# Heads 0 to 3 leave attention undivided, and GpSimd scales them in the gathered rows of the expert layer

## The chip, the cores and the metric

One core of a Trainium2 chip. The metric is the device time of one execution in microseconds (us). TensorE (PE; its weight loads PEld), VectorE (DVE), ScalarE (ACT), GpSimd (POOL) and SyncE (SP) each run their own instructions in order and wait for one another by semaphores; DMA queues move data between DRAM and the core's SBUF.

## The reference

Attention over keys and values that are averaged in groups of 8, then a mixture of 8 experts in which each token takes the one with the largest logit:

```python
k_p = k.reshape(B, H, Sp, pool, D).mean(axis=3)          # B=8, H=8, S=576, D=64, pool=8, Sp=72
v_p = v.reshape(B, H, Sp, pool, D).mean(axis=3)
scores = scale * np.matmul(q, k_p.transpose(0, 1, 3, 2))
scores = scores - np.max(scores, axis=-1, keepdims=True)
attn = np.exp(scores)
attn = attn / (np.sum(attn, axis=-1, keepdims=True) + 1e-09)
x = np.matmul(attn, v_p)                                  # then (4608 tokens) x (512 = 8 heads x 64)
...
logits = x @ w_gate + modality_bias[modality_id]
e_idx = np.argmax(logits, axis=1)                         # softmax of the logits gives gate_w
for e in range(E):                                        # E=8, w1 512x1024, w2 1024x512
    mask = e_idx == e
    h = np.maximum(x[mask] @ w1[e], 0.0)
    out[mask] = gate_w[mask, None] * (h @ w2[e])
```

## The kernel before

**Attention** (about the first 190 us) works on tiles of 128 tokens, 36 in all, in 20 steps: sixteen steps of two tiles, and four "mixed" steps of one tile that holds the last 64 tokens of two batches. For a tile PE computes the scores of all heads (L520, L526, tile sc), DVE takes the maximum and subtracts it (L533, L536, tile sb), ACT exponentiates (L548, L549, tile pe), PE transposes the result in four pieces (L555, tile pp) and a fifth (L567, 16 columns of each pair of heads), ACT copies these to SBUF (L560 pt, L574 pt4), and PE multiplies with the averaged values (a_pe, L590 and L594) into av: for each head 64 columns of the unnormalized output, 8 columns of the unnormalized routing logits (the values' operand holds v times w_gate besides v) and one column with the sum of the exponentials. av is two PSUM banks, heads 0 to 3 and 4 to 7, as two tiles. GpSimd averages k and v beforehand (L296 to L298: three folds, "kp", "vp").

x_dve then divides, in two halves: per half of four heads a tensor_scalar that takes the sum (L610, r), a reciprocal (L612), a product for the 64 columns of each head into the row tile (L614, xb) and one for the logits (L616, lg). Rows go to a DRAM tensor xs, 528 columns a token: 512 of x, then 16 spare ones of which the routing later writes some (the gate's weight).

v_gate (L382 to L387) builds the operand's part with w_gate for a batch: PE into sc, ACT masks two parts (L385, L386), and DVE a third (L387, tile vw4x), which the next mixed step's attention needs. v_operand (L359 to L361) does it for the values; L361 is on GpSimd from the second batch on.

**The order of the work** is written by hand in a loop over the steps n: transposes and exponentials of the step before's first tile (t_pe, t_act), s_act(n, 0), s_pe(n, 1), the fifth transposes with their copies (t4), a_pe of the first old tile, s_dve(n, 1), t_pe of the second old tile, q_pe(n+1, 1), x_dve of the first old tile, s_act(n, 1), s_pe(n+1, 0), s_dve(n+1, 0), a_pe and x_dve of the second old tile, and hooks between them where k, v, v_gate and the first weight splits stand. gap() releases a few small routing operations on DVE ("drip": the logits' maximum and sum, ranks in L717 and so on) between two such operations. So a tile's x_dve at the end of a step is followed on ACT, in program order, by t_act of the next step.

**The expert layer** works on slots of 256 tokens of one expert, about 23 us each, from about 190 us on: gather (L142, GpSimd's DMA queue) takes the slot's rows from xs by index, two tiles of 128 rows, four buffers xg; x_transposes (L153) turns them, ACT and DVE split them in a high and a low part (L155, L156); for each of 8 chunks f of the hidden dimension PE forms hp (L162) and the output (L1143) while DVE and ACT split the weights (L135, L138) that have been loaded. The rows of slot s+1 are gathered at f = 0 of slot s and transposed at f = 5 (slot 1 into 2: gathered at f = 3, transposed at f = 6). The first two slots are gathered inside attention, from a table for its early tokens, and the weights of the first slot are split there.

Of the kernel before, what the change touches and what calls it, by code (L numbers as in the profile page):

```python
# [22 lines left out]
P = 128  # L23
# [7 lines left out]
def kernel(  # L31
# [25 lines left out]
    XW = D + 16  # L57
    NSTAT = NTOK // SLOT
# [87 lines left out]

    def x_transposes(s, xgs, tts=(0, 1)):
        a, b = xh[s % len(xh)], xl[s % len(xl)]
        for tt in tts:
            x = xgs[(2 * s + tt) % len(xgs)]  # L150
            pt = ps_tr.tile([P, ND, P], F32, tag="tr", name=f"xt_{s}_{tt}")
            for d in range(ND):
                nc.tensor.transpose(pt[:, d, :], x[:, d * P:(d + 1) * P], ident)  # L153
# [29 lines left out]
    with ExitStack() as actx:  # L183
# [82 lines left out]
        nc.gpsimd.iota(m_i, pattern=[[-1, NPAIR]], base=P, channel_multiplier=1)  # L266
        nc.vector.tensor_single_scalar(m_i, m_i, NPAIR - 1, op=ALU.bitwise_and)
# [106 lines left out]
        def v_gate(b):  # L374
# [6 lines left out]
            for u in range(2):  # L381
# [5 lines left out]
            nc.vector.tensor_tensor(d4[:, :, HD:HD + E], pg[:, 2, :].rearrange("p (j e) -> p j e", j=NPAIR),  # L387
                                    m4b.to_broadcast([P, NPAIR, E]), op=ALU.mult)
# [151 lines left out]
        def s_act(n, w):  # L540
# [6 lines left out]
            tail = pe[:, 2 * NPAIR * P:].rearrange("p (t s c) -> p t c s", t=2, c=NPAIR)[:, 0:nt, 2 * w:2 * w + 2, :]  # L547
# [28 lines left out]
        def a_pe(t):  # L576
# [3 lines left out]
            av = [ps_av.tile([P, 512], F32, tag=f"av{u}", name=f"av_{t}_{u}") for u in range(2)]  # L580
# [5 lines left out]
            for u in range(2):  # L586
                for gg in range(2):
                    c = 2 * u + gg
                    for hs, y in halves:
                        nc.tensor.matmul(av[u][hs, 2 * VC * gg:2 * VC * (gg + 1)], pt[:, c, hs],  # L590
                                         vw[y][:, c].rearrange("p a x -> p (a x)"), start=(gg == 0), stop=False)
                dst4 = av[u][:, 0:4 * VC].rearrange("p (g x) -> p g x", g=2)[:, :, VC:2 * VC]
# [3 lines left out]
        def x_dve(t):  # L596
# [9 lines left out]
            for u in range(2):  # L606
                avv = av[u][:, 0:4 * VC].rearrange("p (h x) -> p h x", h=4)
                r = ap.tile([P, 4], F32, tag="r", bufs=4, name=f"r_{t}_{u}")
                rb = r.rearrange("p (h o) -> p h o", o=1)
                nc.vector.tensor_scalar(r, avv[:, :, VC - 1], float(POOL), 1e-9 * POOL, op0=ALU.mult, op1=ALU.add)  # L610
                gap(1)
                nc.vector.reciprocal(r, r)  # L612
                gap(1)
                nc.vector.tensor_tensor(xo[:, u * D // 2:(u + 1) * D // 2].rearrange("p (h d) -> p h d", h=4), avv[:, :, 0:HD],  # L614
                                        rb.to_broadcast([P, 4, HD]), op=ALU.mult)
                nc.vector.tensor_tensor(lgs[g][:, gi, 4 * u:4 * u + 4, :], avv[:, :, HD:HD + E],  # L616
                                        rb.to_broadcast([P, 4, E]), op=ALU.mult)
# [139 lines left out]
        def early_table():  # L757
# [31 lines left out]
            ops += [lambda: [gather(s, gidx0, 2 * s, xg, T_EARLY * P) for s in range(EARLY_SLOTS)]]  # L789
# [323 lines left out]
    def part(s):  # L1113
# [62 lines left out]
        def run(fs, tail):  # L1176
            for f in fs:
# [113 lines left out]
```

## Time and profile before

| | us |
|---|---|
| runs shown: median | 640.91 |
| runs shown: all | 640.91, 641.08, 639.33 |
| the profiled execution's own time | 639.47 |
| its span | 637.8 |
| time around the span | 1.67 |

| engine | busy us | share of the span |
|---|---|---|
| PE | 601.1 | 94% |
| DVE | 433.8 | 68% |
| ACT | 343.8 | 54% |
| POOL | 198.9 | 31% |

The busy shares are averages over two stages: attention, in which DVE is close to full for long stretches, and the expert layer, in which PE is. A time line row has the start, the duration, the engine, the line, the operation with its tiles out<-in, and in brackets the idle time ahead of it with what ended it. A row of the groups has the count, the busy time, the mean in ns, and the engine's idle time just ahead with its releasers.

### The profile page before, as it was taken

The numbers are of one execution on the slowest core, as the hardware profiler recorded it, in microseconds if no ns is written. First come the engines' busy times: TensorE is split into PE (matmuls) and PEld (weight loads), VectorE is DVE, ScalarE is ACT, GpSimd is POOL, SyncE is SP. The second block draws the span as 40 slices with busy tenths as digits, with TensorE's granted clock in tenths as the row PEclk, the third lists the DMA queues.
The fourth block names the chain that finished last, engine by engine and source line by source line (L and its number), as shares of the span: only waits on it lengthen the run. The fifth ranks groups of instructions, "written<-read, shape, count | busy, mean of one in ns | idle before, by whom it ended". The sixth has DMA issues, their size and how long they took to land.

```text
span 637.8 us, 12547 instructions
## 1 busy us (share of the span) xinstructions
PE 601.1 (94%) x4223; PEld 544.8 (85%) x4223; DVE 433.8 (68%) x940; ACT 343.8 (54%) x640; POOL 198.9 (31%) x277
## 2 busy tenths in 40 slices
PE   4799898989899999999999999999999999999992
PEld 3699797888798999999999999999999999999881
DVE  4778989999977578666566566656656566656541
ACT  2667566677441455555555555555556555555530
POOL 6689967563000221320320221231131231131230
PEclk9899999999999999999999999999999999999997
DMA  9999979764201901201210461220225410120120
GB/s 255 290 300 337 350 208 362 223 202 143 67 35 51 315 33 36 68 34 35 68 41 28 148 201 51 67 65 8 63 75 180 145 55 17 52 68 18 51 75 17
DMA packets 63406, 77.18 MB, mean 121 GB/s; under 512 B 15455, under 2 KB 42079, under 8 KB 63328
## 3 DMA queue, kind: packets, MB, share of 16 engines
q1 hardware_dynamic: 57168, 55.98, 28.4%
q0 software_dynamic: 6160, 20.26, 9.7%
q8 instruction: 38, 0.62, 0.4%
q14 instruction: 40, 0.33, 0.2%
HBM read 119.94 MB, written 19.45 MB: 219 GB/s over the span
## 4 chain that ended last, share of the span: by engine, by line
PE 76%; DVE 13%; DMA 7%; issue 1%; ACT 1%; SPq 0%; DVEq 0%; ACTq 0%
PE op L1143 30%; PE hp L162 30%; DMA out_dram<-ob,sidx 6%; PE av L590 3%; PE sc L526 3%; PE xt L153 2%; DVE mx L533 2%; DVE sb L536 2%; PE av L594 2%; DVE xb L614 2%; PE pq L501 1%; PE ph L162 1%; PE pp L555 1%; DVE arow L717 1%; DMA k<-in_k_dram 1%
## 5 line engine op out<-in xcount | busy, mean ns | idle before, releaser
L135 ACT CAST hl<-raw 128x1024 fp32r<-128x1024 f32 x138 | 144.8, 1049 | 138.6 <-PE op L1143 136.6
L162 PE MATMUL hp<-xh,hl 128*128 128x256 f32 x1152 | 186.2, 284 | 0.6 <-issue 0.6
L162 PEld LDWEIGHTS hp<-xh,hl 128*128 128x128 f32 x1152 | 166.0, 189 | 11.5 <-issue 1.0
L138 DVE TENSOR_TENSOR hl<-raw,hl 128x1024 fp32r<-128x1024 f32 x144 | 174.8, 1215 | 0.0
L1143 PE MATMUL op<-hl,hh 128*128 128x512 f32 x554 | 173.5, 394 | 0.0
L1129 POOL DMA_INDIRECT out_dram<-ob,sidx x37 | 51.0, 1379 | 369.3 <-DVE ob L1125 260.2
L166 DVE SCALAR_TENSOR_TENSOR hlo<-hp,hh 128x256 fp32r<-128x256 f32 x139 | 58.8, 423 | 136.6 <-ACT hh L164 136.6
L1143 PE MATMUL op<-hl,hlo 128*128 128x512 f32 x277 | 108.4, 391 | 0.0
L1143 PEld LDWEIGHTS op<-hl,hh 128*128 128x128 f32 x554 | 94.8, 189 | 12.1
L162 PE MATMUL hp<-xl,hl 128*128 128x256 f32 x576 | 92.0, 282 | 0.0
L164 ACT ACTIVATE hh<-hp 128x256 fp32r<-128x256 f32 x139 | 53.4, 384 | 49.6 <-PE hp L162 49.6
L162 PEld LDWEIGHTS hp<-xl,hl 128*128 128x128 f32 x576 | 79.0, 190 | 0.0
L1143 PEld LDWEIGHTS op<-hl,hlo 128*128 128x128 f32 x277 | 52.0, 188 | 11.8
L590 PE MATMUL av<-vw,pt 128*128 128x146 f32 (+1 forms) x320 | 50.9, 299 | 4.9 <-DVE lg L616 3.7
L142 POOL DMA_INDIRECT xg<-xs,gidx x40 | 44.2, 1105 | 17.1 <-issue 8.9
L590 PEld LDWEIGHTS av<-vw,pt 128*128 128x128 f32 (+1 forms) x320 | 40.3, 183 | 7.9 <-DVE lg L616 4.9
L526 PE MATMUL sc<-kt,qt 128*128 128x144 f32 x256 | 38.3, 294 | 1.5 <-DVE rs L706 1.1
L526 PEld LDWEIGHTS sc<-kt,qt 128*128 128x128 f32 x256 | 34.1, 195 | 2.4 <-DVE rs L706 1.3
L156 DVE TENSOR_TENSOR xl<-xt,xh 128x512 fp32r<-128x512 f32 x38 | 24.5, 684 | 15.5 <-ACT xh L155 15.5
L560 ACT COPY pt<-pp 128x512 f32<-128x512 f32 x36 | 21.1, 586 | 25.4 <-PE pp L555 25.0
L533 DVE TENSOR_REDUCE mx<-sc 128x8 f32<-128x576 f32 (+1 forms) x40 | 27.7, 692 | 10.0 <-PE sc L526 7.6
L614 DVE TENSOR_TENSOR xb<-av,r 128x256 f32<-128x256 f32 x72 | 30.4, 422 | 1.6
(226 smaller groups left out, 710.5 us busy)
## 6 DMA issues: line engine op xcount, KB each, us to landing
raw<-in_moe_w_dram SPq DMA_DIRECT2D x304, 256.0 KB
xs<-xb SPq DMA_DIRECT2D x16, 528.0 KB
k<-in_k_dram SPq DMA_DIRECT2D x7, 1024.0 KB
v<-in_v_dram SPq DMA_DIRECT2D x7, 1024.0 KB
q<-in_q_dram SPq DMA_DIRECT2D x6, 1024.0 KB
q<-in_q_dram SPq DMA_DIRECT2D x4, 512.0 KB
v<-in_v_dram SPq DMA_DIRECT2D x16, 128.0 KB
xs<-xb SPq DMA_DIRECT2D x8, 132.0 KB
```

Source lines behind the costliest of these rows:

```text
L135: nc.scalar.copy(hl[f][:, 0, :], raw[f])
L138: eng.tensor_sub(hl[f][:, 1, :], raw[f], hl[f][:, 0, :].bitcast(F32))
L142: nc.gpsimd.indirect_dma_start(out=xgs[(2 * s + tt) % len(xgs)], out_offset=None, in_=xs[0:rows, :], in_offset=IndirectOffsetOnAxis(idx[:, ...
L162: nc.tensor.matmul(ph, hl[f][:, w, d * P:(d + 1) * P], x[:, d, :], start=(n == 0 and d == 0), stop=(n == 2 and d == ND - 1))
L164: nc.scalar.activation(hh, ph, AF.Relu)
L166: nc.vector.scalar_tensor_tensor(hlo, ph, 0.0, hh.bitcast(F32), op0=ALU.max, op1=ALU.subtract)
L526: nc.tensor.matmul(dst, qt[:, i, :], kt[b % NB][:, :, h * SPL:(h + 1) * SPL], start=True, stop=True)
L533: nc.vector.reduce_max(mx, scv, axis=AX.X)
L590: nc.tensor.matmul(av[u][hs, 2 * VC * gg:2 * VC * (gg + 1)], pt[:, c, hs], vw[y][:, c].rearrange("p a x -> p (a x)"), start=(gg == 0), sto ...
L614: nc.vector.tensor_tensor(xo[:, u * D // 2:(u + 1) * D // 2].rearrange("p (h d) -> p h d", h=4), avv[:, :, 0:HD], rb.to_broadcast([P, 4, H ...
L1129: nc.gpsimd.indirect_dma_start(out=out[:, :], out_offset=IndirectOffsetOnAxis(idx.bitcast(U32), 0), in_=ob, in_offset=None, bounds_check=N ...
L1143: nc.tensor.matmul(o[tt], l[:, ts_], hl[f][:, w, D:2 * D], start=(f == 0 and n == 0), stop=(f == NF - 1 and n == 2))
```

## The change

1. **x_dve** takes both halves at once: one tensor_scalar for eight sums, one reciprocal, whose result is written into the row itself (columns RX = 520 to 527), one product for all eight heads' logits. The columns of heads 0 to 3 are copied by ACT without division; DVE divides heads 4 to 7 alone. A gap(2) follows.
2. av is one tile over two banks.
3. **scale_half** multiplies, on GpSimd and in place, the first 256 columns of a gathered row tile by the four reciprocals that came with the row: two operations a slot, at f = 3 of the slot before (f = 5 in slot 1), and for slots 0 and 1 right behind their gathers.
4. **v_gate**: the third part is copied out of PSUM by ACT (vg4) and multiplied on GpSimd.
5. The load of v4 lists its rows in another order with the mask to match, and the exponentials of the fifth part are written in the order (t c s) instead of (t s c).

```diff
+    RX = D + 8
...
+    def scale_half(s, xgs):
+        for tt in range(2):
+            x = xgs[(2 * s + tt) % len(xgs)]
+            xv = x[:, 0:D // 2].rearrange("p (h d) -> p h d", h=H // 2)
+            nc.gpsimd.tensor_tensor(xv, xv, x[:, RX:RX + H // 2].rearrange("p (h o) -> p h o", o=1).to_broadcast([P, H // 2, HD]),
+                                    op=ALU.mult)
...
-            src = rows_of(v, b).rearrange("(c r) x -> r c x", r=2 * SPL)[P:]
+            src = rows_of(v, b).rearrange("(c r) x -> c r x", r=2 * SPL)[:, P:, :]
...
-        nc.gpsimd.iota(m_i, pattern=[[-1, NPAIR]], base=P, channel_multiplier=1)
-        nc.vector.tensor_single_scalar(m_i, m_i, NPAIR - 1, op=ALU.bitwise_and)
+        nc.gpsimd.iota(m_i, pattern=[[-16, NPAIR]], base=P, channel_multiplier=1)
+        nc.vector.tensor_single_scalar(m_i, m_i, 16 * (NPAIR - 1), op=ALU.bitwise_and)
...
-            nc.vector.tensor_tensor(d4[:, :, HD:HD + E], pg[:, 2, :].rearrange("p (j e) -> p j e", j=NPAIR),
-                                    m4b.to_broadcast([P, NPAIR, E]), op=ALU.mult)
+            vg4 = ap.tile([P, NPAIR, E], F32, tag="vg4", bufs=1, name=f"vg4_{b}")
+            nc.scalar.copy(vg4, pg[:, 2, :].rearrange("p (j e) -> p j e", j=NPAIR))
+            nc.gpsimd.tensor_tensor(d4[:, :, HD:HD + E], vg4, m4b.to_broadcast([P, NPAIR, E]), op=ALU.mult)
...
-            tail = pe[:, 2 * NPAIR * P:].rearrange("p (t s c) -> p t c s", t=2, c=NPAIR)[:, 0:nt, 2 * w:2 * w + 2, :]
+            tail = pe[:, 2 * NPAIR * P:].rearrange("p (t c s) -> p t c s", t=2, c=NPAIR)[:, 0:nt, 2 * w:2 * w + 2, :]
...
-            av = [ps_av.tile([P, 512], F32, tag=f"av{u}", name=f"av_{t}_{u}") for u in range(2)]
+            av = ps_av.tile([P, 2, 512], F32, tag="av", name=f"av_{t}")
...
-            for u in range(2):
-                avv = av[u][:, 0:4 * VC].rearrange("p (h x) -> p h x", h=4)
-                r = ap.tile([P, 4], F32, tag="r", bufs=4, name=f"r_{t}_{u}")
-                rb = r.rearrange("p (h o) -> p h o", o=1)
-                nc.vector.tensor_scalar(r, avv[:, :, VC - 1], float(POOL), 1e-9 * POOL, op0=ALU.mult, op1=ALU.add)
-                gap(1)
-                nc.vector.reciprocal(r, r)
-                gap(1)
-                nc.vector.tensor_tensor(xo[:, u * D // 2:(u + 1) * D // 2].rearrange("p (h d) -> p h d", h=4), avv[:, :, 0:HD],
-                                        rb.to_broadcast([P, 4, HD]), op=ALU.mult)
-                nc.vector.tensor_tensor(lgs[g][:, gi, 4 * u:4 * u + 4, :], avv[:, :, HD:HD + E],
-                                        rb.to_broadcast([P, 4, E]), op=ALU.mult)
+            avv = av[:, :, 0:4 * VC].rearrange("p u (h x) -> p u h x", h=4)
+            s8 = ap.tile([P, 2, 4], F32, tag="r", bufs=4, name=f"r_{t}")
+            r = xw[:, z, RX:RX + H].rearrange("p (u h) -> p u h", u=2)
+            rb = r.rearrange("p u (h o) -> p u h o", o=1)
+            nc.vector.tensor_scalar(s8, avv[:, :, :, VC - 1], float(POOL), 1e-9 * POOL, op0=ALU.mult, op1=ALU.add)
+            gap(1)
+            nc.vector.reciprocal(r, s8)
+            gap(1)
+            nc.vector.tensor_tensor(lgs[g][:, gi].rearrange("p (u h) e -> p u h e", u=2), avv[:, :, :, HD:HD + E],
+                                    rb.to_broadcast([P, 2, 4, E]), op=ALU.mult)
+            nc.scalar.copy(xo[:, 0:D // 2].rearrange("p (h d) -> p h d", h=4), avv[:, 0, :, 0:HD])
+            nc.vector.tensor_tensor(xo[:, D // 2:D].rearrange("p (h d) -> p h d", h=4),
+                                    avv[:, 1, :, 0:HD], rb[:, 1].to_broadcast([P, 4, HD]), op=ALU.mult)
+            gap(2)
...
+            ops += [lambda: [gather(s, gidx0, 2 * s, xg, T_EARLY * P) for s in range(EARLY_SLOTS)],
+                    lambda: [scale_half(s, xg) for s in range(EARLY_SLOTS)]]
...
+                if f == (5 if s == 1 else 3) and nxt:
+                    scale_half(s + 1, xg)
                 if f == (6 if s == 1 else 5) and nxt:
                     x_transposes(s + 1, xg)
```

What stands on VectorE for the first old tile of step 7 (tile 9; xb5 is its row tile, r_9 its sums, lg_1 its group's logits; lgr, m1, m2 and oh are dripped routing operations), before:

```order
L610 TENSOR_SCALAR r_9_0_1056<-av_9_0_1030 128x4 [waits PE_49]
L666 TENSOR_REDUCE m1_0_989<-lgr_0_987 128x9 [waits DVE_49]
L612 RECIPROCAL r_9_0_1056<-r_9_0_1056 128x4 [waits DVE_49]
L669 TENSOR_TENSOR lgr_0_987<-lgr_0_987,m1_0_989 128x72 [waits DVE_49]
L614 TENSOR_TENSOR xb5_172<-av_9_0_1030,r_9_0_1056 128x256 [waits DVE_49]
L616 TENSOR_TENSOR lg_1_1055<-av_9_0_1030,r_9_0_1056 128x32
L610 TENSOR_SCALAR r_9_1_1064<-av_9_1_1031 128x4 [waits PE_49]
L673 SCALAR_TENSOR_TENSOR lgr_0_987<-lgr_0_987,w8_166 128x72 [waits Activation_49]
L612 RECIPROCAL r_9_1_1064<-r_9_1_1064 128x4 [waits DVE_49]
L674 TENSOR_REDUCE m2_0_990<-lgr_0_987 128x9 [waits DVE_49]
L614 TENSOR_TENSOR xb5_172<-av_9_1_1031,r_9_1_1064 128x256 [waits DVE_49]
L616 TENSOR_TENSOR lg_1_1055<-av_9_1_1031,r_9_1_1064 128x32
```

And in the change, the same tile on the same engine:

```order
L620 TENSOR_SCALAR r_9_1016<-av_9_991 128x8 [waits PE_49]
L678 TENSOR_REDUCE m1_0_950<-lgr_0_948 128x9 [waits DVE_49]
L622 RECIPROCAL xb5_172<-r_9_1016 128x8 [waits DVE_49]
L681 TENSOR_TENSOR lgr_0_948<-lgr_0_948,m1_0_950 128x72 [waits DVE_49]
L624 TENSOR_TENSOR lg_1_1015<-av_9_991,xb5_172 128x64 [waits DVE_49]
L627 TENSOR_TENSOR xb5_172<-av_9_991,xb5_172 128x256 [waits Activation_49]
```

Eight operations have become four, two routing operations that stood inside the tile stand behind it, and the product of heads 4 to 7 (L627) waits for ACT.

On ACT at the end of step 6 and the start of step 7, before (v_gate's two masks, then step 7's pt copy, exponentials and pt4 copies):

```order
L385 ACTIVATE vw1_138<-sc_6_1_1011,m_a_141 128x4x8 [waits PE_49]
L386 ACTIVATE vw1_138<-sc_6_1_1011,m_b_142 128x4x8
L560 COPY pt_11_1137<-pp_11_1132 128x512 [waits PE_49,Activation_49]
L548 ACTIVATE pe_7_1139<-sb_7_0_1092 128x256 [waits DVE_49]
L549 ACTIVATE pe_7_1139<-sb_7_0_1092 128x2x16
L574 COPY pt4_0_135<-sc_7_0_1076 64x128 [waits PE_49,Activation_49]
```

And in the change:

```order
L393 ACTIVATE vw1_138<-sc_6_1_972,m_a_141 128x4x8 [waits PE_49]
L394 ACTIVATE vw1_138<-sc_6_1_972,m_b_142 128x4x8
L396 COPY vg4_3_1055<-sc_6_1_972 128x32
L626 COPY xb5_172<-av_10_1058 128x256 [waits DVE_49,PE_49]
L569 COPY pt_11_1090<-pp_11_1085 128x512 [waits PE_49,Activation_49]
L557 ACTIVATE pe_7_1092<-sb_7_0_1048 128x256
L558 ACTIVATE pe_7_1092<-sb_7_0_1048 128x32
L583 COPY pt4_0_135<-sc_7_0_1032 64x128 [waits PE_49,Activation_49]
```

Two copies have come in ahead of step 7's pt copy; that of the row tile (L626) waits for VectorE's logits product of the same tile (L624).

On GpSimd in the change, at the same v_gate:

```order
L306 TENSOR_TENSOR kp4_4_935<-k4_4_594 64x64 [waits PE_49,Pool_49]
L369 TENSOR_TENSOR vw41_140<-vp4_3_814,m_4_143 128x4x64
L397 TENSOR_TENSOR vw41_140<-vg4_3_1055,m_4_143 128x4x8 [waits Activation_49]
L304 TENSOR_TENSOR v_4_478<-v_4_478 128x2x256 [waits DMAHW1_49]
L305 TENSOR_TENSOR v_4_478<-v_4_478 128x2x128 [waits Pool_49]
```

The second of the two products (L397) is new and waits for ACT's copy vg4; before, the folds of v stood directly behind the first (L361 there).

More of the change, by code (lines that the diff above doesn't have):

```diff
@@ L788, in early_table @@
             ops += finish_table(lambda: psm["t"], C, gidx0, sidx0, "t0")
-            ops += [lambda: [gather(s, gidx0, 2 * s, xg, T_EARLY * P) for s in range(EARLY_SLOTS)]]
+            ops += [lambda: [gather(s, gidx0, 2 * s, xg, T_EARLY * P) for s in range(EARLY_SLOTS)],
+                    lambda: [scale_half(s, xg) for s in range(EARLY_SLOTS)]]
             return ops
```

4 lines of the change are left out of this document (2 added, 2 removed).

## The prediction

> **What bounds the kernel now.** The windows view comes first: for each stretch the span's microseconds, then the busy time of PE, PEld, DVE, ACT and POOL, then clock and DMA.
>
> ```profile
> 56.00:75.00 19.00, 16.23 (x130) 14.20 (x128) 18.63 (x59) 11.60 (x34) 17.67 (x27) 1.00 1.05 365
> 75.00:86.00 11.00, 10.77 (x105) 9.83 (x104) 10.16 (x43) 5.82 (x15) 5.28 (x9) 1.00 0.75 234
> 86.00:116.00 30.00, 27.19 (x214) 24.23 (x213) 28.36 (x89) 20.10 (x55) 24.22 (x40) 1.00 0.96 309
> ...
> 127.00:139.00 12.00, 10.28 (x78) 9.19 (x78) 11.71 (x27) 9.16 (x24) 10.71 (x19) 1.00 0.68 219
> ...
> 147.00:175.00 28.00, 23.65 (x222) 21.26 (x222) 27.13 (x93) 15.74 (x42) 4.24 (x4) 1.00 0.35 108
> ...
> 203.00:592.00 389.00, 389.00 (x2578) 353.96 (x2577) 244.47 (x359) 211.24 (x311) 82.28 (x66) 1.00 0.24 78
> ```
>
> From 203 to 592 TensorE is busy in all of 389.00 us: nothing that VectorE gives up there is worth anything. Four stretches of attention are different: PE is short of full by 2.77, 2.81, 1.72 and 4.35 us, together 11.65, while VectorE is busy in 95 to 98% of them. So **at most 11.65 us** can be won from a lighter VectorE, in 89 us of the span. Between those stretches (75 to 86) PE leads, and there a late ScalarE costs. The groups of instructions (busy us, mean ns, then the engine's idle time ahead) and the waits (total, times, longest) say who holds PE:
>
> ```profile
> L590 PE MATMUL av<-vw,pt 128*128 128x146 f32 (+1 forms) x320 | 50.9, 299 | 4.9 <-DVE lg L616 3.7 <-DVE r L610 0.8 <-ACT pt L574 0.2
> L614 DVE TENSOR_TENSOR xb<-av,r 128x256 f32<-128x256 f32 x72 | 30.4, 422 | 1.6
> L616 DVE TENSOR_TENSOR lg<-av,r 128x32 f32<-128x32 f32 x72 | 12.9, 179 | 0.0
> L612 DVE RECIPROCAL r<-r 128x4 f32<-128x4 f32 x72 | 12.6, 175 | 1.5
> L610 DVE TENSOR_SCALAR r<-av 128x4 f32<-128x4 f32 x72 | 10.8, 151 | 2.9 <-PE av L594 2.9
> L387 DVE TENSOR_TENSOR vw<-sc,m 128x32 f32<-128x32 f32 x7 | 1.3, 182 | 0.4 <-ACT vw L386 0.3
> L361 POOL TENSOR_TENSOR vw<-vp,m 128x256 f32<-128x256 f32 x7 | 4.2, 607 | 7.0 <-PE pk L332 7.0
> L370 ACT COPY vt<-pv 128x256 f32<-128x256 f32 x8 | 2.9, 368 | 0.1
> ```
>
> ```profile
> PE sc L520 <- DVE vw L387: 3.5, 3, 1.3
> ```
>
> x_dve (L610 to L616) holds PE's next attention product for 3.7 us, the gate product in v_gate (L387) its mixed scores for 3.5. Both are edited.
>
> **The change, part by part.** *x_dve.* Its busy time was 2 x (151 + 175 + 422 + 179) = 1.85 us a tile. Now there is one r of 151, one reciprocal of 175, one logits product of 64 columns instead of 32 (not in the trace; between 179 and 422 by the rows, taken as 0.21, nearest the 32-column row) and one product of 422: 0.96. VectorE is rid of **0.89 us a tile**; ScalarE gets a 128x256 copy out of PSUM (368, by L370). But busy time isn't what PE waits for. One tile in which no other operation stood between the steps:
>
> ```profile
> 145.43 0.15 DVE L610 TENSOR_SCALAR r<-av 128x4 f32<-128x4 f32 x1
> ...
> 145.61 0.18 DVE L612 RECIPROCAL r<-r 128x4 f32<-128x4 f32 x1
> ...
> 145.82 0.42 DVE L614 TENSOR_TENSOR xb<-av,r 128x256 f32<-128x256 f32 x1
> ...
> 146.16 0.18 DVE L616 TENSOR_TENSOR lg<-av,r 128x32 f32<-128x32 f32 x1
> ...
> 147.10 1.22 DVE L138 TENSOR_TENSOR hl<-raw,hl 128x1024 fp32r<-128x1024 f32 x1
> ```
>
> Starts follow each other by 0.18 to 0.34, and the tile takes 1.67 from its first start to that of the next thing. After, by the order, the logits product is followed by ScalarE's copy, and VectorE's product of heads 4 to 7 waits for that copy, since all three touch one row tile: 0.18 + 0.21 + 0.21 + the copy 0.37 with some 0.03 on each side + 0.34 = 1.37. The lock step leaves **0.30 of the 0.89**, and with routing operations dripped into the gaps, which fill them before as after, some 0.1. How many tiles lie in the four stretches, the reciprocal of L612 tells, two to a tile (windows of that line alone):
>
> ```profile
> 56.00:75.00 19.00, 1.18 (x7) 1.00 1.05 365
> 86.00:116.00 30.00, 1.87 (x11) 1.00 0.96 309
> 127.00:139.00 12.00, 0.52 (x3) 1.00 0.68 219
> 147.00:175.00 28.00, 1.75 (x10) 1.00 0.35 108
> ```
>
> 31 are 15.5 tiles. I let a dozen count, since elsewhere a max, a table or a PE chain ends last: 12 x 0.1, **-1.2 us**.
>
> *The copy's place on ScalarE.* A step boundary that PE sets:
>
> ```profile
> 54.55 0.60 PE L555 MATMUL pp<-ident,pe 128*128 128x128 f32 x4
> ...
> 55.24 0.59 ACT L560 COPY pt<-pp 128x512 f32<-128x512 f32 x1 [1.71 <-PE pp L555]
> ...
> 56.40 0.55 ACT L574 COPY pt<-sc 64x128 f32<-64x128 f32 x2
> ...
> 57.90 0.27 PE L555 MATMUL pp<-ident,pe 128*128 128x128 f32 x1
> ```
>
> ScalarE sat idle for 1.71 and began the pt copy 0.69 after the attention product before it had ended; two exponentials and the pt4 copies (L574) come behind, on which the next attention product's last part waits, and the boundary lasts 3.35. Now the xb copy stands ahead of that pt copy: it can begin at 0.18 + 0.21 + 0.21 and a hop, some 0.65 after the same point, and ends at 1.02, so all that follows is 0.33 later. With a dripped routing operation ahead of it, more. The pt copies and exponentials leave PE as much to do as it needs at about six of the sixteen boundaries (the kernel has sixteen steps of two tiles), those of the windows between the four stretches: 6 x 0.3 = **+1.8**. At the others VectorE is later than that anyway.
>
> *v_gate.* L387 leaves VectorE (182 ns, x7), ScalarE copies 128x32, and GpSimd multiplies right behind L361. PE waited for L387 because it stood behind other VectorE work; now it waits for a ScalarE copy (under 0.37, by L370) and a GpSimd product (under 0.61, by L361). That is between -3.5 and, if GpSimd is in a 1.27 us fold, +2; GpSimd gets nothing new ahead of it, for it now stands waiting. This waiting has a second result. VectorE's operations on SBUF were long where GpSimd worked beside them:
>
> ```profile
> 109.22 0.60 POOL L361 TENSOR_TENSOR vw<-vp,m 128x256 f32<-128x256 f32 x1
> ...
> 109.33 1.80 DVE L669 TENSOR_TENSOR lgr<-lgr,m 128x72 f32<-128x72 f32 x1
> ...
> 111.62 0.77 PE L590 MATMUL av<-vw,pt 128*128 128x146 f32 x4 [1.31 <-DVE lg L616]
> ```
>
> ```profile
> 154.63 0.23 DVE L669 TENSOR_TENSOR lgr<-lgr,m 128x72 f32<-128x72 f32 x1
> ```
>
> ```profile
> 131.05 2.29 DVE L717 TENSOR_SCALAR arow<-iota_b,rkf 128x128 bf16<-128x128 bf16 x2
> 131.29 0.60 POOL L361 TENSOR_TENSOR vw<-vp,m 128x256 f32<-128x256 f32 x1
> ...
> 131.86 1.26 POOL L296 TENSOR_TENSOR v<-v 128x512 f32<-128x512 f32 x1
> ...
> 136.22 0.77 PE L590 MATMUL av<-vw,pt 128*128 128x146 f32 x4 [1.13 <-DVE lg L616]
> ```
>
> The same L669 took 1.80 beside GpSimd's work and 0.23 without; the two PE waits that follow are 1.31 and 1.13. In the order of the change GpSimd stands still at its gate product from L361 until ScalarE's copy, a few microseconds later, so these operations lose most of their neighbours, and GpSimd makes the folds up later, where it had 7.0 us of waiting. I take **-2.3**, bounds -4 and 0. The Trainium skill, "SBUF — State Buffer", section "Who interferes with whom", has a VectorE instruction with two SBUF inputs and a GpSimd instruction that reads SBUF exclude each other, the second to issue standing still until the first ends; the 1.80 against 0.23 agrees. By that rule each of the four early scales, below, could hold back a weight split for its whole 0.61: an estimate of 2.4 instead of the 0.65 that the sum takes, which would then be +1.5.
>
> *scale_half.* Two GpSimd products of 128x256 a slot, 0.61 each by L361 (bounds 0.61 and 1.27).
>
> ```profile
> L138 DVE TENSOR_TENSOR hl<-raw,hl 128x1024 fp32r<-128x1024 f32 x144 | 174.8, 1215 | 0.0
> ```
>
> ```profile
> 594.40 1.01 POOL L142 DMA_INDIRECT xg<-xs,gidx  x1 [0.31 <-DMA out_dram<-ob,sidx]
> ```
>
> ```profile
> 598.80 0.63 PE L153 MATMUL xt<-ident,xg 128*128 128x128 f32 x4 [0.21 <-DMA xg<-xs,gidx]
> ```
>
> In the last slot the transposes already wait 0.21 for their gather, so one scale shows there: +0.65. Most other slots have six chunks between gather and transposes, and nothing shows. In all of them a scale may meet L138, but PE leads and VectorE idles in 37% of that stretch: 0. Slot 2, gathered late, gets +0.1. Slots 0 and 1 are scaled at about 157 to 160, in a stretch that VectorE bounds and in which L138 runs: half of one L138, **+0.65** (0 to +2.6, the four scales laid against it). Together **+1.4**.
>
> The two-bank av tile makes PE wait once for the whole tile instead of half by half; the next product is half a step away, except where PE waits already, and this is within the 1.37 above. The load order of v4, the mask and the order of the exponential's tail change no count of instructions: 0, since the loads land steps ahead of their folds and the exponentials keep their size; were the tail's write to take longer or shorter by a few ns, it would be lost in ScalarE's idle time.
>
> Sum: -1.2 + 1.8 - 2.3 + 1.4 = **-0.3 us** on a profiled run of 639.47 (span 637.8). That gives 639.2 in the profile's terms and 640.6 from the median of the runs shown (640.91), which lies 1.4 higher; between the two I say **640.0**, and 637 to 643 for this case alone.
>
> **The rivals.** *Faster, 631.* VectorE's load counts and not its chain: 15.5 tiles less 0.89 each is 13.8 us, more than PE's 11.65 us of idling. If three quarters of that idle time go, -8.7, with the terms of ScalarE and the slots a little smaller than mine, it is about 631. For it: VectorE is busy in 95% and more there, so whatever it sheds lets the next max begin sooner, and its new wait for ScalarE lasts about 0.4 us of each tile's 0.89. Against it: the 4.35 us of the last stretch have tables and weight splits that stay. *Slower, 647.* The lock step is paid at all sixteen boundaries: 16 x (0.33 + a dripped operation of some 0.2) = 8.5, less the 2.3; about 640.9 + 6. It decides where VectorE reaches the logits product later than PE has pp ready (0.69 in the quoted boundary): every microsecond of VectorE's lateness then holds ScalarE's queue as well, which before it did not. For it: ScalarE's pt copy, both exponentials and the pt4 copies all stand behind the copy. Against it: ScalarE is busy in 56 to 76% of the stretches only. *No relief, 642.* The change does not do what it says: VectorE waits for each copy as long as it had worked, the stretches keep their idle time, and +1.8 + 1.4 - 1.2 of the rest stay. *Late slots, 645.* The four early scales and slot 2's come last for their transposes: up to 2.6 + 1.2 + 0.65. The Trainium skill, "GPSIMD Engine Reference", puts GpSimd at about half VectorE's speed for products of two inputs and says to use VectorE; L361's 607 against 422 in L614 is milder than that, and the sum uses 607.
>
> **How the numbers follow.** Forecast 0.43 (of it 0.13 faster by over 0.3%, 0.21 within, 0.09 slower; 0.3% is about what a measurement of this kernel can tell from no change), faster rival 0.27, slower 0.17, no relief 0.08 (within 0.05, slower 0.03), late slots 0.05 (slower). Faster 0.13 + 0.26 = 0.39, with 0.01 of that rival inside 0.3%; within 0.21 + 0.01 + 0.05 = 0.27; slower 0.09 + 0.17 + 0.03 + 0.05 = 0.34. The range 632 to 647 leaves out the far half of the two outer rivals.
>
> **What would show it.** Right: PE's idle time in the four stretches falls by 2 to 4 us, the longest waits for x_dve near 111 and 136 shrink below 0.5; VectorE shows a wait for ScalarE of some 0.4 in most tiles; boundaries such as 54.55 to 57.90 last 3.6 to 3.7; the last slot's transposes wait some 0.8 for GpSimd. The faster rival shows as idle time in the stretches under 4 us and short boundaries; the slower one as PE waits for pt copies or pt4 copies at most boundaries. I am wrong if the copy starts much later than 0.65 after the product, or if routing operations do not shorten when GpSimd stands.

## The result and the profile after

The changed kernel takes **651.14 us** (median of 650.81, 650.9, 651.38, 654.34) against 641.0 for the kernel before (639.33 to 641.48, four runs): a ratio of 1.0168, 95% interval 1.0144 to 1.0191, so 10 to 11 us slower. The prediction said 640.0 with 632 to 647. The profiled execution took 650.9 with a span of 649.2.

The windows of the prediction, from the trace of the change (span's us; busy PE, PEld, DVE, ACT, POOL; clock, DMA):

```profile
56.00:75.00 19.00, 16.39 (x123) 14.53 (x122) 14.07 (x36) 11.57 (x34) 17.59 (x31) 1.00 1.06 322
...
86.00:116.00 30.00, 28.45 (x238) 25.60 (x237) 22.38 (x66) 20.14 (x56) 20.03 (x35) 1.00 0.72 223
127.00:139.00 12.00, 10.79 (x100) 9.14 (x98) 8.43 (x25) 8.75 (x23) 7.74 (x14) 1.00 0.68 181
147.00:175.00 28.00, 24.01 (x205) 21.40 (x203) 23.32 (x68) 20.81 (x57) 12.87 (x19) 1.00 0.52 171
203.00:592.00 389.00, 389.00 (x2571) 352.98 (x2571) 247.05 (x382) 206.94 (x307) 107.21 (x96) 1.00 0.24 78
```

The work in a window is no longer the same, since everything sits some 8 us later, but the shares can be read: VectorE is busy in 74, 75, 70 and 83% of stretches in which it was busy in 98, 95, 98 and 97%. It is unloaded, as the change meant. PE is short of full there by 2.61, 1.55, 1.21 and 3.99 us, 9.36 together where it was 11.65: a relief of 2.29, which is what the prediction named as its sign of being right. The time is worse all the same, since the loss lies outside these windows: from 40 to 56 us PE is busy in 14.32 us where it was in 15.97, and from 175 to 195 in 18.52 where it was in 20.00. The groups of x_dve and of the scales, then the waits (total, times, longest):

```profile
L627 DVE TENSOR_TENSOR xb<-av,xb 128x256 f32<-128x256 f32 x36 | 15.3, 425 | 23.4 <-ACT xb L626 22.9 <-issue 0.5
L626 ACT COPY xb<-av 128x256 f32<-128x256 f32 x36 | 13.4, 373 | 41.2 <-DVE lg L624 29.0 <-issue 4.5 <-PE sc L535 3.9
L624 DVE TENSOR_TENSOR lg<-av,xb 128x64 f32<-128x64 f32 x36 | 8.0, 223 | 0.8
L622 DVE RECIPROCAL xb<-r 128x8 f32<-128x8 f32 x36 | 7.2, 200 | 0.8 <-DMA xs<-xb 0.2
L620 DVE TENSOR_SCALAR r<-av 128x8 f32<-128x8 f32 x36 | 5.9, 163 | 21.9 <-PE av L603 21.9
L152 POOL TENSOR_TENSOR xg<-xg 128x256 f32<-128x256 f32 x38 | 31.7, 837 | 38.6 <-DMA xg<-xs,gidx 38.4
```

```profile
POOL v L304 <- DMA v<-in_v_dram: 8.9, 3, 5.2
...
POOL k L304 <- DMA k<-in_k_dram: 6.2, 2, 4.0
...
PE pq L510 <- DMA q<-in_q_dram: 4.4, 3, 1.9
...
PE av L599 <- DVE xb L627: 1.6, 2, 1.3
```

The same waits for loads before:

```profile
POOL v L296 <- DMA v<-in_v_dram: 7.0, 3, 4.2
...
POOL k L296 <- DMA k<-in_k_dram: 2.9, 2, 1.6
...
PE pq L501 <- DMA q<-in_q_dram: 1.1, 1, 1.1
```

Two things stand out. VectorE's product waits for ScalarE's copy 22.9 us in 35 tiles, 0.65 each. And the loads of the first 60 us are late: the waits for loads listed here are 8.5 us longer together (the engines wait side by side, so this is not time lost). Where the time went is seen from when VectorE begins x_dve of a tile (starts of its first operation, us, with the difference from before; tiles are counted from 0 in order of time; the first 30 us vary by 1 to 2 us between kernels that are alike there):

| tile | before | change | load back | load alone | rows apart | rows together | merged |
|---|---|---|---|---|---|---|---|
| 1 | 31.67 | 37.12 (+5.45) | 30.29 (-1.38) | 35.13 (+3.46) | 34.83 (+3.16) | 29.88 (-1.79) | 32.88 (+1.21) |
| 7 | 57.99 | 65.34 (+7.35) | 57.13 (-0.86) | 66.08 (+8.09) | 68.29 (+10.30) | 59.67 (+1.68) | 59.22 (+1.23) |
| 28 | 155.66 | 163.64 (+7.98) | 155.02 (-0.64) | 163.86 (+8.20) | 165.23 (+9.57) | 157.32 (+1.66) | 150.72 (-4.94) |
| 35 | 190.47 | 202.20 (+11.73) | 194.45 (+3.98) | 198.69 (+8.22) | 200.04 (+9.57) | 192.14 (+1.67) | 185.54 (-4.93) |

In the change 7.35 of the 11.73 us are lost by tile 7, in the first 65 us, before attention has come to the stretches that VectorE bounded. From tile 7 to 28 it moves only 0.63, and then 3.75 more. By 155 us, when 18.2 of VectorE's 22.9 us of waiting for the copy are over, this waiting has shown little in the starts.

The granted clock differs in the early part too. From 20 to 30 us before, then from 20 to 30 and 30 to 40 us in the change (the clock is the third figure from the end):

```profile
20.00:30.00 10.00, 8.03 (x47) 6.66 (x48) 7.19 (x16) 5.16 (x15) 7.23 (x12) 0.83 1.10 306
```

```profile
20.00:30.00 10.00, 10.00 (x55) 9.24 (x53) 6.46 (x11) 5.65 (x18) 5.62 (x11) 0.66 0.98 229
30.00:40.00 10.00, 7.62 (x53) 6.74 (x53) 3.31 (x10) 4.76 (x14) 5.58 (x8) 0.83 0.89 269
```

It was 0.83 before and 0.66 in the change, which had 0.83 in the next 10 us too, where before had 1.00. How much of the 7.35 us is waiting for loads and how much the lower clock was not separated.

### The profile page after: what moved, and what is told of

Read it like the earlier page. It is cut to its first block, busy times and chain, and to the rows that moved or that the text cites. A ratio compares the mean times of both kernels' runs of the same rounds, so it can differ in the third digit from the quotient of the medians.

```text
span 649.2 us, 12474 instructions
## 1 busy us (share of the span) xinstructions
PE 609.2 (94%) x4223; PEld 550.4 (85%) x4223; DVE 406.7 (63%) x788; ACT 351.0 (54%) x684; POOL 233.1 (36%) x323
## 3 DMA queue, kind: packets, MB, share of 16 engines
q0 software_dynamic: 6160, 20.26, 9.5%
## 4 chain that ended last, share of the span: by engine, by line
PE 71%; DMA 12%; DVE 5%; issue 4%; ACT 4%; SPq 2%; POOL 0%; POOLq 0%; ACTq 0%; DVEq 0%
PE op L1156 28%; PE hp L170 28%; DMA out_dram<-ob,sidx 6%; PE av L599 3%; DMA q<-in_q_dram 3%; PE sc L535 2%; PE xt L161 2%; PE av L603 2%; DMA v<-in_v_dram 2%; PE ph L170 1%; PE pp L564 1%; PE pq L510 1%; DVE mx L542 1%; DMA raw<-in_moe_w_dram 1%; ACT xb L626 1%
## 5 line engine op out<-in xcount | busy, mean ns | idle before, releaser
L139 DVE TENSOR_TENSOR hl<-raw,hl 128x1024 fp32r<-128x1024 f32 x144 | 176.1, 1225 | 0.0
L1142 POOL DMA_INDIRECT out_dram<-ob,sidx x37 | 52.5, 1418 | 300.2 <-DVE ob L1138 196.4
L152 POOL TENSOR_TENSOR xg<-xg 128x256 f32<-128x256 f32 x38 | 31.7, 837 | 38.6 <-DMA xg<-xs,gidx 38.4
L535 PE MATMUL sc<-kt,qt 128*128 128x144 f32 x256 | 40.7, 306 | 0.5 <-DVE rs L718 0.5
L535 PEld LDWEIGHTS sc<-kt,qt 128*128 128x128 f32 x256 | 36.7, 207 | 1.0 <-DVE rs L718 0.8
L626 ACT COPY xb<-av 128x256 f32<-128x256 f32 x36 | 13.4, 373 | 41.2 <-DVE lg L624 29.0
```

The lines of the kernel that those rows point to most:

```text
L139: eng.tensor_sub(hl[f][:, 1, :], raw[f], hl[f][:, 0, :].bitcast(F32))
L152: nc.gpsimd.tensor_tensor(xv, xv, x[:, RX:RX + H // 2].rearrange("p (h o) -> p h o", o=1).to_broadcast([P, H // 2, HD]), op=ALU.mult)
L535: nc.tensor.matmul(dst, qt[:, i, :], kt[b % NB][:, :, h * SPL:(h + 1) * SPL], start=True, stop=True)
L1142: nc.gpsimd.indirect_dma_start(out=out[:, :], out_offset=IndirectOffsetOnAxis(idx.bitcast(U32), 0), in_=ob, in_offset=None, bounds_check=N ...
```

## The experiments

**1. Load order undone.** In the changed kernel:

```diff
-            src = rows_of(v, b).rearrange("(c r) x -> c r x", r=2 * SPL)[:, P:, :]
+            src = rows_of(v, b).rearrange("(c r) x -> r c x", r=2 * SPL)[P:]
```

with the mask and the order of the exponential's tail back too.

> The changed kernel with part 5 alone undone: v4 is loaded, masked and used in the order of before. Theory L (the other load order delays the loads of the first 40 us, and with them all later work): the 5.5 to 7.5 us that the first six tiles lose go away, the time is 642 to 645. Theory S (the lock step of VectorE and ScalarE in x_dve costs the time): the time stays at 650 to 651. Theory G (the gate product and the scales on GpSimd cost it): 650 to 651.

Measured: 644.73 (before 640.56), ratio 1.0069 (1.0050 to 1.0087). The loss up to tile 7 is gone, and with it 6 us of the 10 to 11; some 4 us stay. Theory L holds for the larger part; S or G must explain the rest. The table shows where the rest lies: between tile 28 and tile 35, where this run goes from -0.64 to +3.98. In that stretch:

```profile
158.23 2.76 DVE L139 TENSOR_TENSOR hl<-raw,hl 128x1024 fp32r<-128x1024 f32 x2
...
162.33 0.23 DVE L624 TENSOR_TENSOR lg<-av,xb 128x64 f32<-128x64 f32 x1
...
162.63 0.37 ACT L626 COPY xb<-av 128x256 f32<-128x256 f32 x1 [3.68 <-issue]
162.90 0.59 ACT L516 COPY qt<-pq 128x512 f32<-128x512 f32 x1
...
163.59 1.09 PE L161 MATMUL xt<-ident,xg 128*128 128x128 f32 x4 [2.88 <-issue]
```

VectorE reaches the tile's logits product (L624) only behind two weight splits (L139) and small operations. ScalarE's row copy waits for that product, 3.68 us, and q's copy (L516) waits behind it in ScalarE's order. The transposes of a slot (L161) take the PSUM buffer that q's copy frees; they begin 0.10 us after it ends, and PE has waited 2.88 us. Before, q's copy began at 159.23. In the change the same wait is there:

```profile
172.51 0.63 PE L161 MATMUL xt<-ident,xg 128*128 128x128 f32 x4 [3.18 <-issue]
```

The clock granted from 158 to 175 us was also lower, 0.90 in this run against 1.00 before.

**2. Load order alone**, put into the kernel before.

```diff
-            src = rows_of(v, b).rearrange("(c r) x -> r c x", r=2 * SPL)[P:]
+            src = rows_of(v, b).rearrange("(c r) x -> c r x", r=2 * SPL)[:, P:, :]
```

> The kernel before with part 5 alone done: load order of v4, mask, order of the exponential's tail. Theory L: 646 to 649, with the loss in the first 50 us. Theories S and G: 641, or 640 since the tail exponentials get shorter.

Measured: 647.51, ratio 1.0120 (1.0099 to 1.0140), all of it lost by tile 7 (+8.09). Part 5 costs about 7 us by itself, with nothing else changed (the mask and the order of the exponential's tail go with the load; experiment 3 changes the load alone). The prediction's edit "at nothing" is the main cause.

**3. Rows apart, and rows together.** Why the other order is slow has two candidates: the change's order begins with a dimension of 4 (before: 16), and it reads rows that lie together. In the kernel before, two other sources of 64 rows (the last eight pooled values of each head are then other ones):

```diff
+            src = rows_of(v, b).rearrange("(c r) x -> c r x", r=2 * SPL)[:, 0:P, :].rearrange("c (q s) x -> c q s x", q=16)[:, :, 0, :]
```

> The kernel before, with v4 loaded from 64 other rows (four groups of 16 rows, each row eight rows behind the one before), so that the first dimension of the load counts 4 as in the change, but no two rows lie together in DRAM. The values of the last eight pooled positions of each head are other ones, so the output and the routing differ. Theory L1 (the first dimension decides over how many DMA engines a load is spread): 192 small packets less, 15263, and the early loss of 4 to 8 us, 645 to 649. Theory L2 (rows that lie together are slow to read): 641, with the attention as early as before.

```diff
+            src = rows_of(v, b)[P:P + 64]
```

> The kernel before, with v4 loaded from 64 rows that lie together in DRAM (the output and the routing differ, as in the run with rows apart); the first dimension then counts 64. Theory L1: small packets as before, 15455, and the time of before, 641. Theory L2: the early loss, 645 to 649.

Measured: 657.06 (1.0239, 1.0213 to 1.0265) and 650.66 (1.0161, 1.0141 to 1.0181). Both totals hold another routing, and so other work in the expert layer, so the two are compared with each other and by the attention part alone: rows apart lose 9.57 us by the end of attention, rows together 1.67, which is there from tile 7 on. The line on DMA packets, of rows apart and of rows together:

```profile
DMA packets 63294, 77.18 MB, mean 118 GB/s; under 512 B 15343, under 2 KB 41967, under 8 KB 63216
```

```profile
DMA packets 63487, 77.18 MB, mean 119 GB/s; under 512 B 15536, under 2 KB 42160, under 8 KB 63409
```

193 small packets less in the first, 12 for each of the 16 loads. (Both counts lie some 80 above what was expected; the queue of the gathers and scatters has 80 packets more in both runs, 6240 in place of 6160, as another routing would have it.) Before and with the load order alone:

```profile
DMA packets 63406, 77.18 MB, mean 121 GB/s; under 512 B 15455, under 2 KB 42079, under 8 KB 63328
```

```profile
DMA packets 63214, 77.18 MB, mean 119 GB/s; under 512 B 15263, under 2 KB 41887, under 8 KB 63136
```

192 less: again 12 a load, as if each load ended on 4 engines in place of 16, with one small packet on each. The semaphore marks in the traces show the same: before and with rows together each of the 16 loads posts 16 landing marks; in the change, with the load order alone and with rows apart it posts one early mark and four landings. What is queued behind lags on four marks too: of a q load issued at 22.28 us in the change, twelve marks land by 28.22 us and four from 32.49 to 33.41, where before all sixteen of it (issued at 17.75) land from 26.33 to 27.64. L1 is right: a load whose first dimension counts 4 is slow even with its rows apart. L2 falls as the main cause; that rows together cost nothing at all is not shown, since that run goes from -1.79 to +1.68 between tiles 1 and 7. The Trainium skill, "DMA: Bandwidth & Descriptors", section "Rules for kernel authors", says L1 outright: an outermost dimension smaller than 16 keeps the whole transfer on at most that many engines. The runs agree, with 12 packets a load and 6 to 8 us.

**4. The same rows in pieces.** The changed kernel, each load as four of 16 rows:

```diff
-                nc.sync.dma_start(t4[64 * z:64 * z + 64], src)
+                for c in range(NPAIR):
+                    nc.sync.dma_start(t4[64 * z + 16 * c:64 * z + 16 * c + 16], src[c])
```

> The changed kernel with its own order of v4 in SBUF, but each load issued as four of 16 rows each (8 issues a batch in place of 2). Theory L1 (a load whose first dimension counts 4 goes to 4 of the DMA engines, one whose first dimension counts 16 to all): the small packets rise by about 16 for each load instead of 4, so to 15263 + 16 x (64 - 4) = 16223, and the early loss mostly goes: 644 to 647, with something lost to 96 more issues on SyncE. Theory L2 (the order of the addresses in DRAM is what is slow): 650 or more.

Measured: 658.59, ratio 1.0280 (1.0255 to 1.0304), slower still. The count came out to the packet:

```profile
DMA packets 64174, 77.19 MB, mean 118 GB/s; under 512 B 16223, under 2 KB 42847, under 8 KB 64096
```

16223 is what L1 said, but the time isn't. Sixty-four issues stand in SyncE's queue instead of 16 (48 more, where the expectation had 96), in front of the other loads. The trace shows what they do there. SyncE's waits for landings at these issues in the first 60 us, the two largest:

```profile
SPq L233 <- DMA v<-in_v_dram: 7.6, 4, 2.6
SPq L233 <- DMA k<-in_k_dram: 6.1, 6, 2.7
```

The loads share eight semaphores, and an issue waits until the load eight places ahead has landed; with eight pieces in a row the large loads behind them go out late. The k load that was issued at 9.56 us before and at 10.21 in the change goes out at 16.07, and from 10 to 20 us the core's DMA share is 0.67 where it was 1.09 in the change. So the price is in SyncE's queue by the trace; no run took it away to confirm that.

**5. What is left: the gate, the scales, the copy.** All of the following have the load order undone. First the gate product back on VectorE (part 4 of the change undone):

```diff
-            vg4 = ap.tile([P, NPAIR, E], F32, tag="vg4", bufs=1, name=f"vg4_{b}")
-            nc.scalar.copy(vg4, pg[:, 2, :].rearrange("p (j e) -> p j e", j=NPAIR))
-            nc.gpsimd.tensor_tensor(d4[:, :, HD:HD + E], vg4, m4b.to_broadcast([P, NPAIR, E]), op=ALU.mult)
+            nc.vector.tensor_tensor(d4[:, :, HD:HD + E], pg[:, 2, :].rearrange("p (j e) -> p j e", j=NPAIR),
+                                    m4b.to_broadcast([P, NPAIR, E]), op=ALU.mult)
```

> As the run with the load order undone, and the gate product back on VectorE (part 4 undone too). Theory G: 2 us or more faster than that run, 640 or less if part 4 is what costs. Theory L, with the working of the prediction that GpSimd's standing still at the gate relieves VectorE: 1 to 2.5 us slower than that run, 643 to 647. Theory S: within 1 us of that run.

Measured: 647.88, ratio 1.0129 (1.0110 to 1.0148): 3 us slower than experiment 1 (644.73). The gate on GpSimd is a gain, as the prediction had it, and theory G falls in this half. The four runs spread from 644.46 to 649.35, and the profiled one is the quickest, no slower than that of experiment 1, so these two traces can't show where the gain lies; the pair in experiment 8 can. Then no scaling of the gathered rows (heads 0 to 3 stay undivided):

```diff
     def scale_half(s, xgs):
-        for tt in range(2):
+        for tt in range(0):
```

> As the run with the load order undone, but the gathered rows are not scaled (scale_half does nothing, so heads 0 to 3 go undivided into the expert layer). The prediction put the scales at 1.4 us: 1.4 us less than that run, in the last slot and between 157 and 165 us. Theory G: 3 us less or more. Theory S: 1 us less or none.

Measured: 642.51, ratio 1.0019 (1.0001 to 1.0038), 2.2 us less than experiment 1. Part of it is one wait in slot 2, whose transposes stand for their scale in experiment 1 and waited for nothing before:

```profile
228.75 1.23 PE L161 MATMUL xt<-ident,xg 128*128 128x128 f32 x8 [1.15 <-POOL xg L152]
```

Another part is the wait of 2.88 us of experiment 1, which is shorter without the scales:

```profile
164.38 0.66 PE L161 MATMUL xt<-ident,xg 128*128 128x128 f32 x4 [1.27 <-ACT qt L516]
```

**6. The copy first.** ScalarE's copy issued ahead of VectorE's sums, so that it waits for nothing of VectorE's:

```diff
+            nc.scalar.copy(xo[:, 0:D // 2].rearrange("p (h d) -> p h d", h=4), avv[:, 0, :, 0:HD])
             nc.vector.tensor_scalar(s8, avv[:, :, :, VC - 1], float(POOL), 1e-9 * POOL, op0=ALU.mult, op1=ALU.add)
```

> The load order undone, and in x_dve ScalarE's copy of heads 0 to 3 issued ahead of VectorE's first operation: it waits for the attention product alone, and VectorE's sums wait for it. Theory S (what is left of the loss, 4 us, is ScalarE's queue standing behind VectorE's logits product; between 160.7 and 163.6 us PE waited 2.88 us because the copy held back ScalarE's q copy, which frees the PSUM tile that the transposes need): that wait goes and the time is 641 to 642.5. Theory C (what is left is the scales on GpSimd beside VectorE's weight splits at 157 to 161 us and in the slots): 644 to 645.

Measured: 643.66, ratio 1.0053 (1.0033 to 1.0074). Only 1 us less than experiment 1, which is not clear of noise (the intervals overlap). The wait of 2.88 us is gone, and tiles 28 to 35 take 2.61 us less than there, but by tile 7 this run is 2.49 us behind the kernel before: in place of ScalarE behind VectorE, VectorE's sums stand behind ScalarE's queue. From 40 to 190 us:

```profile
DVE r L621 <- ACT xb L620: 32.9, 25, 3.3
ACT xb L620 <- PE av L603: 15.1, 16, 2.0
```

Theory S in the form "ScalarE's queue behind VectorE" is too narrow: the hand-over costs in this direction as well. And with slot 1's scales moved out of attention:

```diff
-                    lambda: [scale_half(s, xg) for s in range(EARLY_SLOTS)]]
+                    lambda: scale_half(0, xg)]
...
+                if f == 2:
+                    scale_half(s + 1, xg)
                 if f == 4:
                     x_transposes(s + 1, xg)
```

> As the run with the copy first, and slot 1's two scales moved from attention to chunk 2 of slot 0, two chunks ahead of its transposes. Theory C: 0.7 to 1.5 us less than that run. Theory S: the same within 0.5 us.

Measured: 644.25, ratio 1.0064 (1.0042 to 1.0085), no less. The early scales of slot 1 beside the weight splits are not the loss, so theory C falls there.

**7. The copy last.** VectorE's product ahead of the copy, so that VectorE never waits for ScalarE:

```diff
             nc.vector.tensor_tensor(xo[:, D // 2:D].rearrange("p (h d) -> p h d", h=4),
                                     avv[:, 1, :, 0:HD], rb[:, 1].to_broadcast([P, 4, HD]), op=ALU.mult)
+            nc.scalar.copy(xo[:, 0:D // 2].rearrange("p (h d) -> p h d", h=4), avv[:, 0, :, 0:HD])
```

> The load order undone, and in x_dve VectorE's product of heads 4 to 7 issued ahead of ScalarE's copy: VectorE waits for ScalarE no more, ScalarE waits for the product, and the next attention product waits for the copy. Theory V (what the halves of x_dve on two engines cost is VectorE standing still for the copy, 0.6 us in most tiles): 641 or less, 3 us or more below the run with the load order undone. Theory H (every hand-over costs the same wherever it stands, since tile, copy and product form one chain in any order): 643 to 645.5, as with the copy in the middle or first.

Measured: 641.19 (before 640.89), ratio 1.0014 (1.0000 to 1.0029): 3.5 us less than with the copy in the middle, as theory V had it (its 641 is missed by 0.2), and theory H falls: the place of the copy matters. That VectorE's standing still is the cost, as V says, is not shown. In experiment 1 it stood still 18.0 us before 155 us, and yet tile 28 starts at 155.25 here against 155.02 there; the gain lies between tiles 28 and 35 (191.50 against 194.45 us). There PE's wait for the slot's transposes is 1.67 us in place of 2.88, and the clock granted from 158 to 175 us is 1.00 in place of 0.90. In this kernel no wait of VectorE for a row copy is left; it is ScalarE's copy that waits, and PE a little for pt copies behind it (40 to 190 us):

```profile
ACT xb L628 <- DVE xb L626: 22.1, 15, 3.1
...
PE av L599 <- ACT pt L569: 2.5, 7, 1.0
```

**8. Merged, not split.** No copy and no scales; VectorE takes all eight heads at once:

```diff
-            nc.scalar.copy(xo[:, 0:D // 2].rearrange("p (h d) -> p h d", h=4), avv[:, 0, :, 0:HD])
-            nc.vector.tensor_tensor(xo[:, D // 2:D].rearrange("p (h d) -> p h d", h=4),
-                                    avv[:, 1, :, 0:HD], rb[:, 1].to_broadcast([P, 4, HD]), op=ALU.mult)
+            nc.vector.tensor_tensor(xo.rearrange("p (u h d) -> p u h d", u=2, h=4),
+                                    avv[:, :, :, 0:HD], rb.to_broadcast([P, 2, 4, HD]), op=ALU.mult)
```

> The load order undone, no copy on ScalarE and no scales: VectorE divides all eight heads in one product of 128x512, after one sum, one reciprocal and one logits product for both halves. The gate product stays on GpSimd. Theory S: no lock step, and 5 operations less a tile than before: 638 to 640.5. Theory C: also no scales, so the same. If the time stays at 642 or more, what costs is in the two-bank tile or the gate on GpSimd, and both theories fall.

Measured: **633.38** (before 640.64), ratio 0.9881 (0.9859 to 0.9903), 7 us faster than the kernel before and the fastest here. Its groups:

```profile
L626 DVE TENSOR_TENSOR xb<-av,xb 128x512 f32<-128x512 f32 x36 | 24.4, 679 | 0.0
L624 DVE TENSOR_TENSOR lg<-av,xb 128x64 f32<-128x64 f32 x36 | 8.0, 222 | 0.8
L622 DVE RECIPROCAL xb<-r 128x8 f32<-128x8 f32 x36 | 7.2, 200 | 0.6
L620 DVE TENSOR_SCALAR r<-av 128x8 f32<-128x8 f32 x36 | 5.8, 162 | 18.3 <-PE av L603 18.3
```

One product of 512 columns takes 679 ns, two of 256 took 844. A tile holds VectorE for 162 + 200 + 222 + 679 = 1.26 us, against 1.85 before. In the change it is 163 + 200 + 223 + 425 = 1.01 of work and 22.9 / 36 = 0.64 of waiting: 1.65. Against this, unloading half of the product bought 0.25 us of VectorE's work a tile and cost 0.64 us of its waiting. Its windows show the stretches:

```profile
56.00:75.00 19.00, 17.18 (x128) 15.82 (x128) 17.71 (x48) 11.20 (x33) 16.74 (x28) 0.91 1.05 366
...
86.00:116.00 30.00, 28.37 (x233) 26.34 (x232) 25.37 (x73) 21.89 (x62) 22.86 (x39) 1.00 0.96 306
127.00:139.00 12.00, 11.46 (x94) 10.93 (x93) 10.22 (x27) 10.46 (x29) 7.47 (x13) 1.00 0.68 234
147.00:175.00 28.00, 25.82 (x228) 23.75 (x228) 26.52 (x78) 16.08 (x43) 4.49 (x5) 1.00 0.30 89
```

PE is short of full by 1.82, 1.63, 0.54 and 2.18 us, 6.17 together, where it was 11.65 (the same work lies up to 5 us earlier in them). Last, the same with the gate product back on VectorE, by the diff of experiment 5:

> As the run with merged operations (no copy, no scales, load order undone), with the gate product back on VectorE: the kernel before but for the merged x_dve and the two-bank tile. Theory S (all of the gain is the five operations less): 633 to 635. Theory G2 (a gain of 2 to 3 us comes from GpSimd's standing still at the gate, as the prediction had it): 635.5 to 637.

Measured: 636.98, ratio 0.9940 (0.9919 to 0.9960), 3.6 us slower than merged alone. So the merging by itself gives about 3.8 us on the kernel before, and the gate on GpSimd 3.6 more: G2. The two traces start tile 7 alike (59.22 with the gate on GpSimd, 59.13 without) and tile 28 at 150.72 against 154.72; each has one stretch of lower clock in between (0.91 from 56 to 75 us, 0.88 from 127 to 139). In between, from 56 to 152 us, PE's waits for the gate product (2.2 us) are gone, and operations of VectorE that stood beside GpSimd's work are shorter. With the gate on GpSimd, then on VectorE:

```profile
L728 DVE TENSOR_SCALAR arow<-iota_b,rkf 128x128 bf16<-128x128 bf16 x18 | 7.7, 460 | 0.0
```

```profile
L727 DVE TENSOR_SCALAR arow<-iota_b,rkf 128x128 bf16<-128x128 bf16 x18 | 10.9, 635 | 0.0
```

## Why the prediction was wrong

*The load order (0 in the sum): wrong, and the main cause.* The step that failed is "0, since the loads land steps ahead of their folds". Later loads do; the first 60 us have no such lead, and there the waits for k, v and q grew by 8.5 us together. It measured 6 us (the change less experiment 1) to 7 us (experiment 2). The prediction looked at the count of instructions and not at the form of the transfer, and its windows began at 56 us. In the profile before, GpSimd's 7.0 us of waiting for v and 2.9 for k were to be read, and were passed over.

*The lock step (-1.2 and +1.8): foreseen as a mechanism, wrong in size and place.* Foreseen were the waits of VectorE for ScalarE's copy (0.4 predicted, 0.65 measured) and the copy ahead of the pt copy. One boundary of the change that answers to 54.55 to 57.90:

```profile
61.37 0.60 PE L564 MATMUL pp<-ident,pe 128*128 128x128 f32 x4
...
62.32 0.37 ACT L626 COPY xb<-av 128x256 f32<-128x256 f32 x1 [1.90 <-DVE lg L624]
62.59 0.59 ACT L569 COPY pt<-pp 128x512 f32<-128x512 f32 x1
62.72 0.42 DVE L627 TENSOR_TENSOR xb<-av,xb 128x256 f32<-128x256 f32 x1 [0.49 <-ACT xb L626]
...
65.14 0.60 PE L564 MATMUL pp<-ident,pe 128*128 128x128 f32 x4
```

The pt copy begins 1.22 after the pp transposes where it began 0.69 after, and the boundary lasts 3.77; 3.6 to 3.7 was said. But the terms of x_dve were set at -1.2 and +1.8, +0.6 together. Experiment 1 is 4.2 us above before with the gate's -3 to -3.6 and the scales' +2.2 in it, so x_dve as changed costs 5 to 6. Two terms failed. One is the -1.2, "the lock step leaves 0.30 of the 0.89": with its waiting VectorE's part of a tile went from 1.85 to 1.65, which is 0.20, and the relief of PE in the four stretches bought no time. The other is the +1.8, six boundaries of 0.3: it left out the place where two weight splits stand ahead of x_dve on VectorE. There the copy begins 4.08 us after the attention product in the change (L603 ends at 167.47), holds q's copy, and PE waits 3.18 us; in experiment 1 it is 2.88, of which 1.27 stay without the scales. "The copy starts much later than 0.65 after the product" was the prediction's own sign of being wrong. Experiment 7 shows that 3.5 us of the loss hang on the order of copy and product; how the 5 to 6 us divide between this one wait, the lower clock behind it, VectorE's standing still and the routing operations that now stand behind the product was not separated.

*The gate (-2.3): right.* Experiments put it at -3.2 (experiment 5 against 1) and -3.6 (the merged pair of experiment 8). The reason holds too, by the rows of that pair (7.7 in place of 10.9). The operation that took 1.80 beside GpSimd's work now stands at

```profile
118.42 0.30 DVE L681 TENSOR_TENSOR lgr<-lgr,m 128x72 f32<-128x72 f32 x1
```

*The scales (+1.4): right in sign, 2.2 measured;* but they lie in slot 2 (1.15) and at the first transposes (2.88 against 1.27), while the last slot's 0.65 did not show, and moving two of the early ones changed nothing.

*The rivals.* "Slower, 647" named the lock step and came nearest in sign, with a wrong main cause; its condition, that VectorE's lateness holds ScalarE's queue, is seen at the one place above. "Faster" held that VectorE's load counts. For the change that was wrong, but experiment 8 shows that it was not the load that was wrong: with the operations merged, no hand-over and the gate on GpSimd, PE gets back half of the idle time.

## What to carry to other kernels

Before moving half of an operation to another engine, price the hand-over from the trace: here 0.25 us of saved work a tile bought 0.64 us of waiting, and joining two half operations into one on the same engine was worth more. Then look at what stands behind the handed-over operation in its new queue: most of the waiting cost little, and one copy that held up the next one cost PE about 3 us. Read the order of dimensions of every edited transfer as closely as the instructions: the same bytes with 4 in front instead of 16 cost more than all other edits together (net), and the count of small packets on the profile's page tells it at a glance. A bundle of edits is to be measured one by one; in this one a gain of 3 us lay under three losses.

## What the runs showed that was not expected

A product of 128x512 out of PSUM took 679 ns on VectorE where two of 128x256 took 422 each, so joining them saves 165 ns. GpSimd's scale took what its nearest row said (607) in most cases, but 837 in the mean, since some of the 38 ran up to 1.6 us (minimum, median and maximum in ns):

```profile
L152 POOL TENSOR_TENSOR xg<-xg x38: 607/614/1595, 165.6 to 608.1; 128x256 f32<-128x256 f32 x38
```

The last slot's scale cost nothing because PE comes to the transposes later: in experiment 1 they begin at 602.68 us, 6.51 after the first gather's issue and just behind the second scale, which ends at 602.31; without scales (experiment 5) they begin 6.50 us after it, and before 5.10. Why PE comes later stays open.
